# Reordering the first batch of a fused attention and gated-MLP kernel, and opening three units ahead of each block

## The chip, the cores and the metric

The kernel runs on one core of a Trainium2 chip. A core has a matrix engine (TensorE, PE in the profile, with its weight loads as PEld), a vector engine (VectorE, DVE), a scalar engine with function tables (ScalarE, ACT), a general engine (GpSimd, POOL) and a queue engine (SyncE, SP) that does nothing but issue transfers. Each works through its own instructions in order, and they wait for one another by semaphores. Sixteen DMA engines move data between the chip's memory and the on-core buffers. The metric is the device time of one execution in microseconds (us). Before the change the median of three runs is 176.78 us (176.47 to 177.16).

## The reference

Two layers, one behind the other. The first is attention over 4 batches, 8 heads, 768 positions and head width 64, in which a position sees the 128 positions up to itself and the first 4 positions of the sequence (the sinks):

```python
scores = scale * np.matmul(q, k.transpose(0, 1, 3, 2))
keep = is_sink | in_window                 # 4 sinks, window of 128
a = softmax(np.where(keep, scores, -1e9))  # over the last axis
x = np.matmul(a, v)                        # then heads side by side: (4, 768, 512)
```

The second is a gated MLP with mixing along the sequence:

```python
h = gelu_tanh(x @ w_in)                    # 512 -> 1024
u, v = h[..., :512], h[..., 512:]
v_n = (v - mean) / sqrt(var + 1e-6) * g_ln # over the 512 of v
v_s = einsum('ts,bsd->btd', w_sg, v_n) + b_sg[None, :, None]   # 768 x 768
out = x + (u * v_s) @ w_out                # 512 -> 512
```

## The kernel before

**Pairs.** The attention works on 16 pairs of heads, n = 0 to 15, four to a batch (HP = 4). For a pair, `load` (L86) brings k, q and v from memory as 32-bit floats, 384 KB each, through SP's queue; three buffers for each of the three. `cast` (L97) makes them 16-bit. `columns` (L195) turns k or q by six TensorE transposes into a PSUM bank and copies the bank out, on VectorE or ScalarE. `score(n, groups)` (L222) makes one, two or all of the pair's three groups of scores, of two key blocks each, in one of two double banks; ScalarE takes the exponential at L248. In the first four pairs, and in group 0 of pair 4, the band mask is put in beforehand: `begin_scores` (L213) fills the bank with large negative numbers by a matmul. Later pairs are masked after the exponential by `keep_band` (L250): group 0 on VectorE (L257), groups 1 and 2 on GpSimd, two selects for each group (L265, L267). `values(n, c)` (L274) multiplies one half of the pair's rows by v and divides on VectorE (L299, L300). `turn_x(n, eng)` (L304) turns the pair's result and copies it (L312 on VectorE).

**Blocks.** Behind each batch's four pairs stands a block, `hidden(b, between)` (L527). It has 14 units: six of the v half (`hidden_v`, L328), each over 128 rows, and eight of the u half (`hidden_u`, L339). A unit of the v half has four matmuls, one for each pair of the batch; `open_v` (L319) may do the first three beforehand (L325), and `hidden_v` then adds the fourth (L332), takes the gelu on ScalarE (L334) and the statistics on VectorE (L336, L337). Behind unit 7 stand `inverse_root` (L350) and the first `normalise` (L369), and one more `normalise` behind each later unit; the dictionary `between` puts other steps behind a unit of a given number. A block's later steps, `spatial` (L376: the matmuls with w_sg at L382, then L385 and L388 on VectorE) and `project` (L408), go onto the list `fillers`; `fill` takes them one by one in the pair loop of the next batch (L638 to L681), and the last batch's are taken at the end.

**Banks.** Two double banks hold scores. Four banks hold everything else (columns, values, x, hidden units, spatial, projections); a new tile gets the bank of an earlier one, and waits until that has been read.

**First batch.** Its steps are written out by hand in L554 to L634, and each engine works in that order. POOL issues the weights' loads, which turn 32-bit floats into 16-bit ones on the way: the v half of w_in (L585), the u half (L592), the two halves of w_sg (L600), and w_out (L632). So a weight is asked for when POOL has done the casts written ahead of it. SP's queue passes three gates: `hold_loads(i, behind)` (L82) issues a tiny copy that reads `behind`, so that SP waits there until `behind` has landed. The first gate stands behind w_in's v half and ahead of pair 4's k and q and of b_sg; the second behind w_in's u half and ahead of pair 4's v; the third behind w_sg's first half and ahead of pairs 5 and 6. w_sg is turned by `turn_weights` (L178): three of six columns of blocks at the end of the first block, three in the loop's first round.

Of the kernel before, what the change touches and what calls it, by code (L numbers as in the profile page):

```python
# [8 lines left out]
F32 = mybir.dt.float32  # L9
BF16 = mybir.dt.bfloat16  # L10
# [8 lines left out]
def kernel(  # L19
# [57 lines left out]

    raw = {}

    gates = consts.tile([1, 4, 16], BF16, name="gates")  # L80

    def hold_loads(i, behind):  # L82

# [13 lines left out]
    def cast(n, which, eng):  # L97
        src = raw.pop((n, which))
        if which == "v":
            eng.tensor_copy(v_bufs[n % NV][:, :, :, 0:64], src)  # L100
            return
        dst = work.tile([128, NT, 128], BF16, name=which + "_bf")
        eng.tensor_copy(dst.rearrange("p t (h d) -> p h t d", h=2), src)  # L103
        flat[n, which] = dst
# [65 lines left out]
    def turn_g():  # L170
        ps = bank([128, 512], F32, "gps")
        nc.tensor.matmul(ps[:, 0:KU], g_rows, iden4, start=True, stop=True)
        V.tensor_copy(g_sb, ps[:, 0:KU])
# [15 lines left out]
    def bank(shape, dtype, name):  # L189
        return ps_m.tile(shape, dtype, name=name, tag="m")  # L190
# [4 lines left out]
    def columns(n, which, eng):  # L195
        src = flat.pop((n, which))
        ps = bank([128, NT, 128], BF16, which + "ps")
        for t in range(NT):
            nc.tensor.transpose(ps[:, t, :], src[:, t, :], iden)  # L199
        dst = work.tile([128, S], BF16, name=which + "T")  # L200
        o, i = dst.rearrange("c (p t) -> c p t", t=NT), ps.rearrange("c t p -> c p t")
        if eng is A:
            A.copy(o, i)  # L203
        else:
            eng.tensor_copy(o, i)  # L205
        (kTs if which == "k" else qTs)[n] = dst
# [15 lines left out]
    def score(n, *groups):  # L222
        kT, qT = kTs[n], qTs[n]
        if 0 in groups:
            exps[n] = work.tile([128, HT, 1024], BF16, name="ex", bufs=3)
        for g in groups:
            if (n, g) not in scores:
                begin_scores(n, g)
            sc = scores.pop((n, g))
            w, dark = 0, darkened(n, g)  # L230
            for j in (2 * g, 2 * g + 1):
                n_q = min(256, S - 128 * j)
                for l in range(2):
                    rows = slice(64 * l, 64 * l + 64)
                    nc.tensor.matmul(sc[:, 512 * l + w:512 * l + w + n_q],  # L235
                                     kT[rows, 128 * j:128 * (j + 1)],
                                     qT[rows, 128 * j:128 * j + n_q], start=not dark,
                                     stop=not dark or j % 2 == 1)
                w += n_q
            if g == HT - 1:  # L240
                for a in range(4):
                    for l in range(2):
                        rows = slice(64 * l, 64 * l + 64)
                        nc.tensor.matmul(
                            sc[32 * a:32 * (a + 1), 512 * l + w:512 * (l + 1)], kT[rows, 0:32],
                            qT[rows, 128 * (a + 2):128 * (a + 3)], start=True, stop=True,
                            tile_position=(64 * l, 32 * a))
            A.activation(out=exps[n][:, g, :], in_=sc, func=AF.Exp, scale=scale)  # L248
# [67 lines left out]

    hvs = {}

    def open_v(b, j):  # L319
        if j == 0:  # L320
            v_alls[b] = work.tile([128, NT, DF], F32, name="v_all", tag="v_all", bufs=1)
            mvs[b] = small.tile([128, NT, 2], F32, name="mv", bufs=2)
        hvs[b, j] = bank([128, 512], F32, "hv")
        for c in range(KD - 1):
            nc.tensor.matmul(hvs[b, j], xT[b][:, c, 128 * j:128 * (j + 1)],  # L325
                             w_in_sb[:, c, DF:], start=(c == 0), stop=False)

# [240 lines left out]
    load(3, "v")  # L568


    score(0, 0, 1)
    columns(1, "k", V)
    columns(1, "q", V)
# [2 lines left out]
    cast(2, "q", G)  # L576
    score(0, 2)
    score(1, 0, 1)
    turn_g()
    columns(2, "k", A)  # L580
    columns(2, "q", V)
    cast(3, "k", G)
# [1 line left out]
    score(1, 2)  # L584
    load_w_in(slice(DF, d_ff))  # L585
    cast(1, "v", G)
    values(0, 0)
    values(0, 1)
    score(2, 0, 1)
    columns(3, "k", A)  # L590
    cast(2, "v", G)
    load_w_in(slice(0, DF))  # L592
    turn_x(0, V)
    columns(3, "q", V)
    score(2, 2)
    values(1, 0)
    values(1, 1)
    score(3, 0, 1)
    cast(3, "v", G)
    load_w_sg()  # L600
    values(2, 0)
    turn_x(1, V)
    values(2, 1)
    score(3, 2)

    hold_loads(0, w_in_sb[0:1, 0, DF:DF + 16])
    load(HP, "k")
    load(HP, "q")
    nc.sync.dma_start(out=b_bc, in_=moe_b_sg.partition_broadcast(128))
    hold_loads(1, w_in_sb[0:1, 0, 0:16])  # L610
    load(HP, "v")
    hold_loads(2, wsg_sb[0][0:1, 0, 0:16])
    for n in (HP + 1, HP + 2):
        for which in "kqv":
            load(n, which)
    cast(HP, "k", G)
    cast(HP, "q", G)
    values(HP - 1, 0)
    turn_x(HP - 2, V)
    values(HP - 1, 1)  # L620
    open_v(0, 0)
    turn_x(HP - 1, V)
    open_v(0, 1)
    cast(HP, "v", G)
    for which in "kqv":
        load(HP + 3, which)
# [11 lines left out]
    for n in range(HP, NP):  # L638
        todo = valued < n - 1
        block = n % HP == 0 and n > HP  # L640
        if HP + 3 < n + 3 < NP:
            for which in "kqv":
                load(n + 3, which)
        if n not in exps:
            score(n, 0, 1)
        if n == HP:
            for si in range(3, NT):
                turn_weights(si, V)
        keep_band(n, 0, V)
        keep_band(n, 1, G)  # L650
        if todo:
            values(n - 1, 0)
        fill(1 if todo else 2)
        if n + 1 < NP and not block:
            columns(n + 1, "k", A)
        score(n, 2)
        keep_band(n, 2, G)
        if todo:
            values(n - 1, 1)
        if QUOTA[n] > 2 and todo:  # L660
            fill()
        if n + 1 < NP and not block:
            columns(n + 1, "q", A if todo else V)
        if n + 2 < NP:
            for which in "kqv":
                cast(n + 2, which, G)
        if block:
            open_v(n // HP - 1, 0)
        if QUOTA[n] > 1:
            fill()  # L670
        if todo:
            turn_x(n - 1, V)
        if block:
            open_v(n // HP - 1, 1)
        valued = n - 1
        if block:
            hidden(n // HP - 1, {1: [lambda: values(n, 0)], 3: [lambda: values(n, 1)],
                                 5: [lambda: columns(n + 1, "k", A)], 6: [lambda: turn_x(n, V)],
                                 8: [lambda: columns(n + 1, "q", A)],
                                 LAST: [lambda: score(n + 1, 0, 1), lambda: fill(2)]})  # L680
            valued = n  # L681
    fill()
# [1 line left out]
    values(NP - 1, 1)  # L684
    fill(len(fillers) - 3)
    open_v(B - 1, 0)
    turn_x(NP - 1, V)
    open_v(B - 1, 1)
    seen = {}
    hidden(B - 1, {2: [lambda: seen.update(c=count_good())],  # L690
                   LAST: [lambda: fill(3)]})
# [42 lines left out]
```

## Time and profile before

| | us |
|---|---|
| runs, median of 3 | 176.78 |
| the profiled execution | 177.16 |
| its span | 175.3 |
| PE busy | 160.0 |
| DVE busy | 134.3 |
| ACT busy | 113.5 |
| POOL busy | 73.7 |

The span runs from the program's first instruction to its last; the execution's own time is 1.86 us longer. A row of the timeline has a start, a length, the engine, the line, the operation, the tile written and the tiles read, how many instructions it joins (x6), and in brackets how long the engine had been idle before it and who ended that. A row of the chain of waits has a start, a length and what the chain went through: an engine's instruction, a transfer (DMA), or a queue (SPq). Matmuls are pipelined, so the length of a row of matmuls has a tail beyond the moment at which the next can begin. In this execution the granted TensorE clock was 0.997 of full speed.

### The profile page before, as it was taken

The page shows a single profiled execution, that of the slowest core. Times are in us where ns is not written, and L with a number is a line of the kernel's source. Part 1 is how long each engine was busy: PE and PEld are TensorE (multiplying, and loading weights), DVE is VectorE, ACT ScalarE, POOL GpSimd, SP SyncE. Part 2 cuts the span into 40 slices and gives each one's busy share as a digit, 9 for nine tenths or more (in the row PEclk, how much of TensorE's full clock was granted, in tenths as well). Part 3 has the DMA queues.
Part 4 walks back from the last instruction along what each step waited for, and adds up shares of the span by engine and source line. Part 5 has one row for each costly group of instructions (what it writes and reads, how often), then busy time and mean ns, then how long its engine had stood idle before and what let it go on. Part 6 is the DMA issues. An engine that isn't in the chain of part 4 may idle for free.

```text
span 175.3 us, 4180 instructions
## 1 busy us (share of the span) xinstructions
PE 160.0 (91%) x1620; PEld 96.3 (55%) x1638; DVE 134.3 (77%) x322; ACT 113.5 (65%) x153; POOL 73.7 (42%) x110
## 2 busy tenths in 40 slices
PE   3989989879999999999999999999999999999960
PEld 3535654347666665565567655564676645555530
DVE  6655646997889998699689993997989979868620
ACT  2187774768986698768886875779787437621130
POOL 6344840125799989600269987000494300000000
PEclk9999999999999999999999999999999999999998
DMA  4999999998999989900099949100300130040352
GB/s 146 291 316 232 187 175 184 305 288 227 299 215 291 251 248 331 251 1 4 14 326 299 286 130 337 54 0 4 120 4 0 39 144 2 0 180 2 120 183 77
DMA packets 40355, 28.75 MB, mean 164 GB/s; under 512 B 26484, under 2 KB 37240, under 8 KB 40328
## 3 DMA queue, kind: packets, MB, share of 16 engines
q1 hardware_dynamic: 36992, 25.11, 50.7%
q0 software_dynamic: 2912, 2.77, 10.1%
q10 hardware_dynamic: 424, 0.53, 0.9%
q8 instruction: 15, 0.25, 0.6%
q14 instruction: 12, 0.10, 0.2%
HBM read 24.81 MB, written 6.29 MB: 177 GB/s over the span
## 4 chain that ended last, share of the span: by engine, by line
PE 59%; DVE 17%; DMA 13%; ACT 3%; issue 3%; POOL 1%; SPq 1%; POOLq 0%; DVEq 0%; ACTq 0%
PE vs L382 13%; PE hu L344 10%; PE o_ps L413 9%; DMA q_sb<-in_q_dram 9%; PE sc L235 5%; DMA w_in_sb<-in_moe_w_in_dram 4%; PE av L291 4%; PE hv L325 4%; DVE gv L385 3%; DVE qT L205 3%; DVE x L300 2%; DVE gT L388 2%; PE qps L199 2%; PE kps L199 2%; PE hv L332 2%
## 5 line engine op out<-in xcount | busy, mean ns | idle before, releaser
L248 ACT ACTIVATE ex<-sc 128x1024 bf16<-128x1024 f32 x48 | 47.5, 1024 | 11.7 <-PE sc L235 7.5
L382 PE MATMUL vs<-wsgT,vn 128*128 128x384 bf16 x192 | 35.3, 326 | 0.1
L265 POOL TENSOR_SCALAR_AFFINE_SELECT ex<-ex 128x512 bf16<-128x512 bf16 x24 | 16.0, 666 | 37.4 <-ACT ex L248 30.6
L382 PEld LDWEIGHTS <-vn 128*128 128x128 bf16 x192 | 17.9, 97 | 10.6 <-issue 0.3
L413 PE MATMUL o_ps<-w_out_sb,gT 128*128 128x512 bf16 x83 | 23.1, 379 | 0.5
L344 PE MATMUL hu<-xT,w_in_sb 128*128 128x384 bf16 x128 | 22.4, 326 | 0.0
L334 ACT ACTIVATE v_all<-hv 128x512 f32<-128x512 f32 x24 | 13.8, 596 | 13.0 <-PE hv L332 12.2
L385 DVE SCALAR_TENSOR_TENSOR gv<-vs,g_sb,b_bc 128x384 bf16<-128x384 f32 x32 | 19.6, 612 | 3.4 <-PE vs L382 3.1
L336 DVE BATCH_NORM_STATS2 st<-v_all 128x6 f32<-128x512 f32 x24 | 16.1, 671 | 5.0 <-ACT v_all L334 5.0
L103 POOL CAST k_bf<-k_sb 128x768 bf16<-128x768 f32 x15 | 12.7, 845 | 16.9 <-PE hu L344 10.4
L325 PE MATMUL hv<-w_in_sb,xT 128*128 128x512 bf16 x68 | 19.2, 379 | 0.5 <-DVE xT L312 0.3
L300 DVE TENSOR_TENSOR x<-av,rcps 128x384 bf16<-128x384 f32 x32 | 17.8, 557 | 1.1
L347 ACT ACTIVATE uT<-hu 128x384 bf16<-128x384 f32 x32 | 15.8, 492 | 4.2 <-PE hu L344 3.6
L388 DVE TENSOR_TENSOR gT<-gv,uT 128x384 bf16<-128x384 bf16 x32 | 16.7, 522 | 2.2 <-DVE gv L385 0.5
L422 ACT COPY o_sb<-o_ps 128x512 f32<-128x512 f32 x13 | 7.4, 593 | 14.8 <-PE o_ps L419 13.3
L235 PE MATMUL sc<-qT,kT 64*128 64x256 bf16 x192 | 15.7, 264 | 1.4 <-DVE qT L205 0.9
L103 POOL CAST q_bf<-q_sb 128x768 bf16<-128x768 f32 x15 | 14.3, 953 | 4.9 <-DMA q_sb<-in_q_dram 4.9
L344 PEld LDWEIGHTS <-w_in_sb 128*128 128x128 bf16 x128 | 12.2, 98 | 7.5
L203 ACT COPY kT<-kps 128x768 bf16<-128x768 bf16 x15 | 12.0, 799 | 6.4 <-PE kps L199 6.3
L291 PE MATMUL av<-v_sb,ex 128*128 128x65 bf16 x352 | 15.9, 194 | 0.0
L291 PEld LDWEIGHTS <-ex 128*128 128x128 bf16 x352 | 13.0, 98 | 4.1 <-issue 2.1
L100 POOL CAST v_sb<-v_sb 128x768 bf16<-128x768 f32 x15 | 13.3, 890 | 3.3 <-DMA v_sb<-in_v_dram 2.6
(90 smaller groups left out, 237.5 us busy)
## 6 DMA issues: line engine op xcount, KB each, us to landing
k_sb<-in_k_dram SPq DMA_DIRECT2D x16, 384.0 KB, 6.2
v_sb<-in_v_dram SPq DMA_DIRECT2D x16, 384.0 KB, 6.7
out_dram<-o_sb SPq DMA_DIRECT2D x23, 256.0 KB, 2.8
q_sb<-in_q_dram SPq DMA_DIRECT2D x15, 384.0 KB, 5.6
wsg_sb<-in_moe_w_sg_dram POOLq DMA_DIRECT2D x2, 576.0 KB, 11.3
w_in_sb<-in_moe_w_in_dram POOLq DMA_DIRECT2D x2, 512.0 KB, 7.5
w_out_sb<-in_moe_w_out_dram POOLq DMA_DIRECT2D x1, 512.0 KB, 9.3
q_sb<-in_q_dram ACTq DMA_DIRECT2D x1, 384.0 KB, 4.6
```

The lines of the kernel that those rows point to most:

```text
L103: eng.tensor_copy(dst.rearrange("p t (h d) -> p h t d", h=2), src)
L235: nc.tensor.matmul(sc[:, 512 * l + w:512 * l + w + n_q], kT[rows, 128 * j:128 * (j + 1)], qT[rows, 128 * j:128 * j + n_q], start=not dark, ...
L248: A.activation(out=exps[n][:, g, :], in_=sc, func=AF.Exp, scale=scale)
L291: nc.tensor.matmul(av[:, m, l, :], probs(j, l, half), v_sb[:, l, j, :], start=first, stop=False)
L300: V.tensor_mul(x_sb[b][:, hp, HT * c:HT * (c + 1), :].rearrange("p i (l d) -> p i l d", l=2), av[:, :, :, 0:64], rcp.to_broadcast([128, HT ...
L325: nc.tensor.matmul(hvs[b, j], xT[b][:, c, 128 * j:128 * (j + 1)], w_in_sb[:, c, DF:], start=(c == 0), stop=False)
L336: V.bn_stats(out=st, in_=v_alls[b][:, j, :])
L344: nc.tensor.matmul(h_ps[:, 0:NH], w_in_sb[:, c, 128 * f:128 * (f + 1)], xT[b][:, c, NH * n:NH * (n + 1)], start=(c == 0), stop=(c == KD - 1))
L382: nc.tensor.matmul(vs[:, 0:NH], vns[b][:, si, 128 * f:128 * (f + 1)], wsgT[:, si, cols], start=(si == 0), stop=(si == NT - 1))
L385: V.scalar_tensor_tensor(out=gv, in0=vs[:, 0:NH], scalar=g_sb[:, f:f + 1], in1=b_bc[:, cols], op0=ALU.mult, op1=ALU.add)
L388: V.tensor_mul(gTs[b][:, f, cols], gv, uTs[b][:, f, cols])
L413: nc.tensor.matmul(o_ps, gTs[b][:, c, rows], w_out_sb[:, c, :], start=(c == 0), stop=(c == KU - 1 and not by_act))
```

## The change

The order of the steps in the first batch is changed, and with it which transfers are asked for when:

- `score(2, 0)`, and the k columns of pair 3, stand ahead of `values(0, ...)`; `score(2, 1)` and `score(2, 2)` ahead of `values(1, ...)`, as does the first part of pair 3's scores; `turn_x(0)` stands behind the q columns of pair 3.
- `turn_x(1)` and `turn_x(2)` copy on ScalarE instead of VectorE; `turn_g` stands later.
- the load of w_in's u half stands behind the cast of pair 3's v, directly ahead of w_sg's.
- SP has two gates instead of three. The first reads pair 3's v as it was loaded, and pair 4's k, q and v and b_sg stand behind it; the second reads w_sg's first half, and pairs 5 and 6 stand behind it.
- three units of the first block are opened instead of two: the matmuls of pairs 0 and 1 for all three, then `turn_x(3)`, then those of pair 2.

In the later blocks two units are opened ahead of `turn_x` and a third behind it (before: one ahead, one behind), the filler at that place stands ahead of them, `columns(n + 1, "q")` stands behind unit 7 (before: 8), and `turn_x(n)` behind unit 9 (before: 6). The last batch's block is opened in the same way.

```diff
-    gates = consts.tile([1, 4, 16], BF16, name="gates")
+    gates = consts.tile([1, 4, 8], F32, name="gates")
...
-    def open_v(b, j):
-        if j == 0:
+    def open_v(b, j, cs=range(KD - 1)):
+        if j == 0 and 0 in cs:
...
-        hvs[b, j] = bank([128, 512], F32, "hv")
-        for c in range(KD - 1):
+        if (b, j) not in hvs:
+            hvs[b, j] = bank([128, 512], F32, "hv")
+        for c in cs:
...
+    landed = raw[3, "v"]
     score(0, 0, 1)
...
     score(1, 0, 1)
-    turn_g()
...
     load_w_in(slice(DF, d_ff))
     cast(1, "v", G)
+    score(2, 0)
+    columns(3, "k", A)
     values(0, 0)
     values(0, 1)
-    score(2, 0, 1)
-    columns(3, "k", A)
+    score(2, 1)
+    score(2, 2)
+    columns(3, "q", V)
     cast(2, "v", G)
-    load_w_in(slice(0, DF))
     turn_x(0, V)
-    columns(3, "q", V)
-    score(2, 2)
+    score(3, 0, 1)
     values(1, 0)
     values(1, 1)
-    score(3, 0, 1)
+    score(3, 2)
     cast(3, "v", G)
+    load_w_in(slice(0, DF))
     load_w_sg()
+    turn_x(1, A)
     values(2, 0)
-    turn_x(1, V)
     values(2, 1)
-    score(3, 2)
-
-    hold_loads(0, w_in_sb[0:1, 0, DF:DF + 16])
+    turn_g()
+
+    hold_loads(0, landed[0:1, 0, 0, 0:8])
     load(HP, "k")
     load(HP, "q")
+    load(HP, "v")
     nc.sync.dma_start(out=b_bc, in_=moe_b_sg.partition_broadcast(128))
-    hold_loads(1, w_in_sb[0:1, 0, 0:16])
-    load(HP, "v")
-    hold_loads(2, wsg_sb[0][0:1, 0, 0:16])
+    hold_loads(1, wsg_sb[0][0:1, 0, 0:16].bitcast(F32))
...
     values(HP - 1, 0)
-    turn_x(HP - 2, V)
     values(HP - 1, 1)
-    open_v(0, 0)
+    turn_x(HP - 2, A)
+    for j in range(3):
+        open_v(0, j, (0, 1))
     turn_x(HP - 1, V)
-    open_v(0, 1)
+    for j in range(3):
+        open_v(0, j, (2,))
...
+        if QUOTA[n] > 1:
+            fill()
         if block:
             open_v(n // HP - 1, 0)
-        if QUOTA[n] > 1:
-            fill()
+            open_v(n // HP - 1, 1)
         if todo:
             turn_x(n - 1, V)
         if block:
-            open_v(n // HP - 1, 1)
+            open_v(n // HP - 1, 2)
...
-                                 5: [lambda: columns(n + 1, "k", A)], 6: [lambda: turn_x(n, V)],
-                                 8: [lambda: columns(n + 1, "q", A)],
+                                 5: [lambda: columns(n + 1, "k", A)],
+                                 7: [lambda: columns(n + 1, "q", A)], 9: [lambda: turn_x(n, V)],
...
     open_v(B - 1, 0)
+    open_v(B - 1, 1)
     turn_x(NP - 1, V)
-    open_v(B - 1, 1)
+    open_v(B - 1, 2)
```

## The prediction

> **What bounds the kernel now.** I read the page first: its busy shares, then its DMA slices.
>
> ```profile
> span 175.3 us, 4180 instructions
> PE 160.0 (91%) x1620; PEld 96.3 (55%) x1638; DVE 134.3 (77%) x322; ACT 113.5 (65%) x153; POOL 73.7 (42%) x110
> ...
> DMA  4999999998999989900099949100300130040352
> ```
>
> TensorE is the bound, 15.3 us short of the whole span. The DMA engines are full in every slice (of 4.4 us) from the second to the ninth, that is from 4.4 to 39 us, and again later; their first gap is where the first batch ends. So I read the chain of waits in order of time for the first 45 us:
>
> ```profile
> 17.84 7.86 DMA w_in_sb<-in_moe_w_in_dram
> ...
> 25.72 0.59 SPq L84
> ...
> 27.03 9.81 DMA q_sb<-in_q_dram
> ...
> 36.99 0.84 POOL q_bf L103
> ```
>
> The chain runs through the v half of w_in (landed at 17.84 + 7.86 = 25.70), the gate behind it (L84), pair 4's q (landed at 36.84) and its cast. The timeline shows what TensorE and ScalarE wait for there; brackets hold the idle time before an instruction and who ended it:
>
> ```profile
> 17.19 1.94 ACT L248 ACTIVATE ex<-sc 128x1024 bf16<-128x1024 f32 x2 [1.00 <-PE sc L235]
> ...
> 21.77 1.94 ACT L248 ACTIVATE ex<-sc 128x1024 bf16<-128x1024 f32 x2 [0.78 <-PE sc L235]
> ...
> 24.73 1.02 ACT L248 ACTIVATE ex<-sc 128x1024 bf16<-128x1024 f32 x1 [1.02 <-PE sc L244]
> ...
> 25.80 0.24 PE L297 MATMUL av<-vsink,ex 128*128 128x65 bf16 x2 [0.74 <-ACT ex L248]
> ...
> 29.50 1.68 ACT L334 ACTIVATE v_all<-hv 128x512 f32<-128x512 f32 x3 [2.45 <-PE hv L332]
> ...
> 32.97 1.46 PE L344 MATMUL hu<-xT,w_in_sb 128*128 128x384 bf16 x8
> ...
> 35.39 0.51 PE L199 MATMUL kps<-iden,k_bf 128*128 128x128 bf16 x6 [0.96 <-POOL k_bf L103]
> ...
> 37.87 0.51 PE L199 MATMUL qps<-iden,q_bf 128*128 128x128 bf16 x6 [0.67 <-POOL q_bf L103]
> ...
> 40.82 1.17 PE L181 MATMUL wps<-iden,wsg_sb 128*128 128x128 bf16 x18
> ```
>
> After 46 us TensorE has few waits left. GpSimd's timeline shows why a gain before 45 us need not survive:
>
> ```profile
> 21.08 0.74 POOL L162 DMA_DIRECT2D w_in_sb<-in_moe_w_in_dram  x1
> ...
> 21.82 0.83 POOL L100 CAST v_sb<-v_sb 128x768 bf16<-128x768 f32 x1
> ...
> 39.56 0.85 POOL L100 CAST v_sb<-v_sb 128x768 bf16<-128x768 f32 x1 [1.75 <-DMA v_sb<-in_v_dram]
> ...
> 44.77 0.83 POOL L100 CAST v_sb<-v_sb 128x768 bf16<-128x768 f32 x1 [0.67 <-PE vs L382]
> ...
> 45.55 0.77 POOL L176 DMA_DIRECT2D w_out_sb<-in_moe_w_out_dram  x1
> ...
> 46.93 0.63 POOL L265 TENSOR_SCALAR_AFFINE_SELECT ex<-ex 128x512 bf16<-128x512 bf16 x1 [0.62 <-ACT ex L248]
> ...
> 48.54 0.64 POOL L265 TENSOR_SCALAR_AFFINE_SELECT ex<-ex 128x512 bf16<-128x512 bf16 x1 [0.28 <-PE vs L382]
> ...
> 49.51 0.94 POOL L103 CAST k_bf<-k_sb 128x768 bf16<-128x768 f32 x1
> ...
> 50.59 0.50 PE L199 MATMUL kps<-iden,k_bf 128*128 128x128 bf16 x6
> ```
>
> Pair 5's v cast at 44.77 waited for its load (the engine named had long been done). Behind it stand the issue of w_out, pair 4's band selects and pair 6's k cast, which ends at 49.51 + 0.94 = 50.45; TensorE turns that tile at 50.59. From the landing of v5 to there GpSimd idles only 0.62 + 0.28 = 0.90 us.
>
> **The change, part by part, first batch.** *Score groups ahead of values.* The three exponential waits are 1.00 + 0.78 + 1.02 = 2.80. Now score(2,0) runs while the exponential of (1,2) is under way, so the first goes; the next two shrink to an estimated 0.4 each, since score(3,0) still waits for the columns of pair 3's q. The last exponential ends near 23.8 in place of 25.75. TensorE's 0.74 goes. What is late next is the v half at 25.70, a little ahead of where the first open_v stood before. So TensorE opens the three units at about 25.9, and the first hu comes between 31.6 (everything on time) and 32.97 (nothing gained).
>
> *Two turn_x copies on ScalarE*: 0.8 each, by the nearest copy of a tile of that size (row below), inside its 2.45 of idle before the first gelu: nothing. *turn_g later*: two tiny matmuls and a copy, moved into the same stretch: nothing. *Gate shapes and one gate fewer*: one issue less on SP: nothing.
>
> ```profile
> L203 ACT COPY kT<-kps 128x768 bf16<-128x768 bf16 x15 | 12.0, 799 | 6.4 <-PE kps L199 6.3
> ...
> q_sb<-in_q_dram SPq DMA_DIRECT2D x15, 384.0 KB, 5.6
> ```
>
> *Loads held by v3.* v3 had landed by its cast at 21.82, so the gate is passed 25.72 - 21.82 = 3.9 us sooner, and SP issues k4, q4, v4 and b_bc then. Pair 4's casts come well ahead of 35.39 and 37.87, and TensorE's 0.96 + 0.67 = 1.63 go. From hu to wps takes 40.82 - 32.97 = 7.85 before, so 6.2 after: TensorE reaches wps between 37.8 and 39.2.
>
> *u half and w_sg later.* On POOL the u half now stands behind the cast of v3, that is at 22.6 in place of 21.08, and w_sg behind it, 0.74 later. What is late next is w_sg's second half:
>
> ```profile
> L168 POOL DMA_DIRECT2D wsg_sb<-in_moe_w_sg_dram x2: 738/752/767, 22.6 to 23.3; - x2
> ...
> DMA to landing us min/median/max: 7.6/9.4/13.3
> ```
>
> It landed at 23.3 + 13.3 = 36.6. Now k4, q4, v4 and b_bc go ahead of or beside it, in DMA engines that have no room. Bounds: 36.6 (not delayed), and 39.5, where before all of these loads had landed (the cast of v4 at 39.56). I take 38.5: most of them do go ahead. So wps moves from 40.82 to about 38.5, by 2.3, with 1.3 and 3.0 as ends.
>
> *What takes most of that back.* The same bytes precede v5 in the same full engines, so I hold v5 where it was, at 44.7. GpSimd then goes from its cast through w_out and four selects to k6 without its 0.90 of idle, and no sooner. TensorE waits for pair 4's selects in values(4,0) and for k6 at 50.59. So the gain after 51 us is at most 0.90; the least, if v5 comes 0.9 later, is nothing. I take 0.80: the sequence is the one on the trace, and its casts vary (0.83 to 0.94).
>
> One rule of the Trainium skill speaks against this part: "DMA: Bandwidth & Descriptors", section "Queues, rings and completion order", says each DMA engine takes turns between the queue rows that have work. By it, SP's k4 slows POOL's v half from the moment the gate opens; the 9.81 us of q4 beside w_sg, against the 5.6 that is the median of the q loads (row above), agrees. By the rule alone the v half would land about 1 us later, and the sum would come out the same, because GpSimd's bound above is the tighter.
>
> **The blocks.** The rows, at pairs 8, 12 and the last batch:
>
> ```profile
> 76.93 0.50 PE L308 MATMUL xps<-iden,x 128*128 128x128 bf16 x6
> ...
> 70.49 0.65 PE hv L325 x3
> ...
> 69.53 0.33 PE L308 MATMUL xps<-iden,x 128*128 128x128 bf16 x3
> ...
> 70.15 0.34 PE L308 MATMUL xps<-iden,x 128*128 128x128 bf16 x3 [0.29 <-DVE x L300]
> ...
> 71.14 0.11 PEld L332 LDWEIGHTS <-xT 128*128 128x128 bf16 x2 [0.50 <-DVE xT L312]
> ...
> 113.82 0.33 PE L308 MATMUL xps<-iden,x 128*128 128x128 bf16 x3
> ...
> 114.32 0.34 PE L308 MATMUL xps<-iden,x 128*128 128x128 bf16 x3 [0.17 <-DVE x L300]
> ...
> 141.17 0.59 PE L308 MATMUL xps<-iden,x 128*128 128x128 bf16 x6
> ...
> 78.39 0.53 DVE L312 COPY xT<-xps 128x768 bf16<-128x768 bf16 x1
> ...
> 78.90 3.41 PE L344 MATMUL hu<-xT,w_in_sb 128*128 128x384 bf16 x20
> ...
> 81.24 2.83 DVE L372 TENSOR_SCALAR vn<-v_all,mv,y 128x512 bf16<-128x512 f32 x6
> ```
>
> A unit's three opening matmuls take 0.65. Six transposes in a row take 0.50 with a tail of about 0.16, so three take 0.17. At pair 8 the second three start 0.62 after the first: 0.45 of waiting for x. A second unit opened ahead gives x 0.65 more: the 0.45 go. The wait for xT behind it stays, as one unit covers it before and after. At pair 12 the turn of x(12) waits 114.32 - 113.82 - 0.17 = 0.33; moved behind unit 9 it no longer does. In the last batch the six transposes took 0.59 against 0.50, and the xT copy queued behind an output add; I take 0.16 for both, with 0 and 0.3 as ends. Sum 0.45 + 0.33 + 0.16 = 0.94. Opening a unit ahead delays the first gelu of the block by 0.65 - 0.45 = 0.2; VectorE's normalised tiles still end (81.24 + 2.83 = 84.07) ahead of the spatial matmuls behind two projections, so nothing. The fill that moves ahead of open_v does the same work earlier: nothing. The q transposes at unit 7 instead of 8: same work, nothing.
>
> **Sum.** The profiled execution took 177.16 (span 175.3 and 1.86 around it), 0.38 over the median of 176.78. 177.16 - 0.80 - 0.94 = 175.42; against the median, 175.04.
>
> **Rivals.** *(a) GpSimd does not bind*, because v5 lands sooner or its selects do: then w_sg's landing and VectorE's wsgT copies set the shift, 1.3 to 2.3, and the time is 176.78 - 0.94 - 1.8, about 174.0. For it: SP passes its last gate with less in its queue. Against: the DMA share shows no free engine before 40 us.
>
> *(b) The first batch gives nothing*: v5 lands 0.9 or more later, since k5's gate now waits behind w_sg's first half, which itself stands later. Time 176.78 - 0.94 = 175.8. For it: w_sg asked 0.74 later. Against: v4 and b_bc keep SP's queue filled meanwhile.
>
> *(c) Slower: the bank of the late turn.* turn_x behind unit 9 puts its copy on VectorE behind the inverse root and three normalisations. Without the copy ahead, normalising starts at 81.24 - 0.53 = 80.7; three take 1.42, the copy 0.53: the PSUM bank is free at 82.7. The last hu unit starts at 78.90 + 4 x 0.65 = 81.5, less 0.45. If it is given that bank, one of four, TensorE waits 1.6 in each of two blocks: 175.04 + 3.2 = 178.2. It decides when this unit, not one after it, gets the bank. Against: the other three banks come back as soon as a gelu has read them, and a bank that is free sooner may be taken first.
>
> *(d) w_sg's second half lands after 42.5*, with everything SP asked ahead of it: the first batch then loses 1.7 and more, 177.5.
>
> **How the numbers follow.** Forecast 0.52; (a) 0.13; (b) 0.18; (c) 0.10; (d) 0.07: GpSimd's idle is on the trace, while (a), (c) and (d) each need an order of transfers or banks that no row shows. A change of 0.5%, 0.9 us, is about what this measurement can tell: faster is below 175.9, slower above 177.66. The forecast's own range is 174.4 to 175.8. The forecast, but for 0.02 at its edge, and (a) are faster; (b) lies at the bound, and 0.06 of it is faster, 0.12 same; (c) is slower; (d) is split. That makes faster 0.69, same 0.18, slower 0.13. The range runs from 173.8, just below (a), to 177.0, between (b) and (d); it leaves out (c), most of (d) and a little of (a), 0.19 in all.
>
> **What would show it.** Right: no wait above 0.3 at the exponentials of pair 2, k4 and q4 transposes without wait, wps starting near 38.5 and behind a wsg landing, a wait of TensorE for GpSimd between 46 and 51 us, the k6 transposes near 49.8, and no wait for x at pairs 8 and 12. Wrong: wps later than 40 us, v5's cast away from 44.8, or a hu unit that waits for VectorE's xT copy near 81 or 118 us.

## The result, and the profile after

The changed kernel takes 174.83 us (median of 6 runs), the kernel before 176.84 on the same chip: a ratio of 0.9881, with a 95% interval from 0.9856 to 0.9905. By this ratio it is faster by 2.1 us. The ratio, like those below, leaves out executions that took well over the kernel's shortest (here one of the six, 179.34 at a granted clock of 0.979, where the others had 0.991 to 0.998), so the two medians lie a little less apart, 2.0. The profiled execution took 174.74. The head of its page:

```profile
span 173.0 us, 4178 instructions
PE 160.5 (93%) x1621; PEld 96.9 (56%) x1638; DVE 132.6 (77%) x320; ACT 114.1 (66%) x155; POOL 74.5 (43%) x110
```

TensorE's busy time is nearly the same (160.0 before) and the span is 2.3 shorter. The timeline of ScalarE and TensorE in the first batch, after the change (start, length, engine, line, what, and in brackets the idle time before it and who ended it; `...` marks rows left out; lines from L325 on are one higher here than before):

```profile
18.16 1.94 ACT L248 ACTIVATE ex<-sc 128x1024 bf16<-128x1024 f32 x2 [0.31 <-PE sc L235]
20.98 1.94 ACT L248 ACTIVATE ex<-sc 128x1024 bf16<-128x1024 f32 x2 [0.88 <-PE sc L235]
23.61 1.02 ACT L248 ACTIVATE ex<-sc 128x1024 bf16<-128x1024 f32 x1 [0.69 <-PE sc L244]
...
29.69 1.57 ACT L335 ACTIVATE v_all<-hv 128x512 f32<-128x512 f32 x3 [0.76 <-PE hv L333]
...
26.63 1.64 PE L326 MATMUL hv<-w_in_sb,xT 128*128 128x512 bf16 x5
...
32.51 1.46 PE L345 MATMUL hu<-xT,w_in_sb 128*128 128x384 bf16 x8
33.81 0.50 PE L199 MATMUL kps<-iden,k_bf 128*128 128x128 bf16 x6
...
35.44 0.50 PE L199 MATMUL qps<-iden,q_bf 128*128 128x128 bf16 x6
...
38.38 1.17 PE L181 MATMUL wps<-iden,wsg_sb 128*128 128x128 bf16 x18
...
43.49 2.22 PE L383 MATMUL vs<-wsgT,vn 128*128 128x384 bf16 x9 [1.37 <-DVE wsgT L186]
...
50.11 0.50 PE L199 MATMUL kps<-iden,k_bf 128*128 128x128 bf16 x6
```

Pair 4's k and q are turned without a wait, and TensorE is at wps 2.44 ahead of before (38.38 against 40.82). Then it waits 1.37 for VectorE's copies of w_sg, and at pair 6's k transposes only 0.48 is left (50.11 against 50.59). This wait stands where before had none. What VectorE and GpSimd do there, after the change:

```profile
37.66 3.93 DVE L373 TENSOR_SCALAR vn<-v_all,mv,y 128x512 bf16<-128x512 f32 x6
...
41.82 0.82 DVE L146 COPY mask<-mask 128x512 bf16<-128x512 bf16 x1
...
42.95 1.41 DVE L186 COPY wsgT<-wps 128x768 bf16<-128x768 bf16 x3
...
40.48 0.83 POOL L103 CAST k_bf<-k_sb 128x768 bf16<-128x768 f32 x1 [1.13 <-DMA k_sb<-in_k_dram]
41.67 0.83 POOL L103 CAST q_bf<-q_sb 128x768 bf16<-128x768 f32 x1 [0.36 <-PE wps L181]
43.31 0.83 POOL L100 CAST v_sb<-v_sb 128x768 bf16<-128x768 f32 x1 [0.81 <-DMA v_sb<-in_v_dram]
...
47.93 0.64 POOL L265 TENSOR_SCALAR_AFFINE_SELECT ex<-ex 128x512 bf16<-128x512 bf16 x1 [1.84 <-PE vs L383]
```

And before, with TensorE's first opened unit:

```profile
26.75 0.38 PE L325 MATMUL hv<-w_in_sb,xT 128*128 128x512 bf16 x1
...
38.26 3.33 DVE L372 TENSOR_SCALAR vn<-v_all,mv,y 128x512 bf16<-128x512 f32 x6
...
41.83 0.29 DVE L146 COPY mask<-mask 128x512 bf16<-128x512 bf16 x1
...
43.44 1.49 DVE L186 COPY wsgT<-wps 128x768 bf16<-128x768 bf16 x3 [0.94 <-PE wps L181]
```

Before, VectorE waited 0.94 for TensorE's wps; now it comes to w_sg's copies straight from its own masks, 0.49 ahead of before. GpSimd casts pair 5's v at 43.31 in place of 44.77, and idles 1.84 ahead of its second pair of selects: no wait for what it hands over holds the first batch.

The blocks after the change, on the timeline of TensorE and VectorE:

```profile
69.42 0.50 PE L308 MATMUL xps<-iden,x 128*128 128x128 bf16 x6
...
78.38 2.76 PE L345 MATMUL hu<-xT,w_in_sb 128*128 128x384 bf16 x16
81.08 0.61 PE L235 MATMUL sc<-qT,kT 64*128 64x256 bf16 x8
...
140.35 0.50 PE L308 MATMUL xps<-iden,x 128*128 128x128 bf16 x6
...
81.74 0.55 DVE L312 COPY xT<-xps 128x768 bf16<-128x768 bf16 x1
```

At pair 8 the six transposes come in one piece where before they came three and three; in the last batch they take 0.50 in place of 0.59. The copy of the late turn is at 81.74, behind three normalised tiles; by then the units of hu have run through without a gap.

To see where time goes, I compare the starts of the same ScalarE instructions in two traces: the first exponential of a pair, and the last copy of an output. The table says how many us each kernel is ahead of the kernel before at these places (+: behind). The labels are those of the experiments; "after" is the changed kernel as it was first measured (the expectations call this the first look), and e13 is the same kernel again.

| start in the kernel before | 44.9 (pair 4) | 49.2 (pair 5) | 55.2 (pair 6) | 66.3 (pair 8) | 84.2 (pair 9) | 121.4 (pair 13) | 168.4 (last copy) |
|---|---|---|---|---|---|---|---|
| after | 2.44 | 0.48 | 0.48 | 0.76 | 1.17 | 1.46 | 1.75 |
| e13, the same kernel again | 2.55 | 1.18 | 1.18 | 1.46 | 1.87 | 2.17 | 2.46 |
| e1, first batch alone | 2.62 | 0.87 | 0.77 | 1.01 | 1.23 | 1.22 | 1.35 |
| e2, blocks alone | 0.80 | 0.09 | 0.09 | 0.09 | 0.50 | 0.80 | 0.96 |
| e4, two units opened | 2.51 | 1.76 | +0.52 | +0.24 | 0.17 | 0.47 | 0.76 |
| e10, and product from PSUM | 2.44 | 2.36 | 1.96 | 2.18 | 2.59 | 2.50 | 2.32 |
| e11, GpSimd waits | 2.13 | 1.54 | 1.43 | 1.67 | 2.08 | 2.38 | 2.66 |
| e12, PSUM but in the last batch | 2.13 | 2.05 | 0.33 | 0.28 | 0.69 | 0.60 | 0.68 |
| e5, old gates | 0.73 | 0.73 | 0.73 | 1.01 | 1.42 | 1.72 | 2.01 |
| e9, old order of scores | 2.54 | 1.12 | 1.12 | 1.12 | 1.53 | 1.83 | 1.99 |
| e15, old gates, PSUM | 0.13 | 0.15 | 0.15 | 0.34 | 0.75 | 0.66 | 0.74 |

Two traces of one kernel differ by 0.7 between pairs 4 and 5 and then keep that difference to the end. From pair 13 to the last copy "after" gains 0.29: 0.16 is there at the first output behind the last block (at 152.85 before, 151.23 after), and 0.13 comes behind that, in e1 too, whose last block is as before. One trace shows where time goes; what a part is worth is read from the times.

### The profile page after: what moved, and what is told of

It is laid out like the page before. It is cut to its first block, busy times and chain, and to the rows that moved or that the text cites. A ratio compares the mean times of both kernels' runs of the same rounds, so it can differ in the third digit from the quotient of the medians.

```text
span 173.0 us, 4178 instructions
## 1 busy us (share of the span) xinstructions
PE 160.5 (93%) x1621; PEld 96.9 (56%) x1638; DVE 132.6 (77%) x320; ACT 114.1 (66%) x155; POOL 74.5 (43%) x110
## 4 chain that ended last, share of the span: by engine, by line
PE 78%; DVE 14%; issue 2%; POOL 1%; ACT 1%; POOLq 0%; DVEq 0%; ACTq 0%
PE vs L383 15%; PE o_ps L414 11%; PE hu L345 9%; PE hv L326 8%; PE av L291 7%; PE sc L235 7%; PE xps L308 3%; PE hv L333 3%; DVE qT L205 3%; PE kps L199 3%; PE qps L199 2%; PE sc L218 2%; DVE vn L373 2%; PE av L297 2%; DVE st L337 2%
## 5 line engine op out<-in xcount | busy, mean ns | idle before, releaser
L335 ACT ACTIVATE v_all<-hv 128x512 f32<-128x512 f32 x24 | 13.3, 599 | 11.3 <-PE hv L333 10.0
L326 PE MATMUL hv<-w_in_sb,xT 128*128 128x512 bf16 x68 | 18.7, 379 | 0.3
L300 DVE TENSOR_TENSOR x<-av,rcps 128x384 bf16<-128x384 f32 x32 | 17.8, 557 | 1.1
L100 POOL CAST v_sb<-v_sb 128x768 bf16<-128x768 f32 x15 | 14.0, 934 | 9.2 <-DVE vn L373 6.8
```

The lines of the kernel that those rows point to most:

```text
L300: V.tensor_mul(x_sb[b][:, hp, HT * c:HT * (c + 1), :].rearrange("p i (l d) -> p i l d", l=2), av[:, :, :, 0:64], rcp.to_broadcast([128, HT ...
```

## Experiments

The expectations speak of theories V, G, P and R. V: VectorE's chain, from the first gelu over statistics, inverse root, normalised tiles and masks to w_sg's copies, sets the first batch's end. G: GpSimd's casts and selects do, as in the prediction. P: VectorE's instructions with both inputs in on-core buffers wait out GpSimd's. R: such a long instruction waits for something else.

**The two halves of the change.** e1 is the changed kernel with the later blocks as before; e2 is the kernel before with the blocks changed.

```diff
 e1
-            open_v(n // HP - 1, 0)
-            open_v(n // HP - 1, 1)
+        if block: open_v(n // HP - 1, 0)     # fill() and turn_x(n - 1, V) behind it, then open_v(.., 1)
-        7: columns(n + 1, "q"), 9: turn_x(n, V)
+        6: turn_x(n, V), 8: columns(n + 1, "q")
```

> The first batch as changed, the later blocks as before. Theory V (VectorE's chain from the first gelu over statistics, inverse root, normalising and masks to its wsgT copies sets the first batch's end): pair 6's k transposes at 50.1 us as in the changed kernel, TensorE waiting about 1.4 us for VectorE's wsgT copies, the time 0.5 to 0.8 under before. Theory G (the prediction's: GpSimd's casts and selects set it): the same place, reached by a wait for GpSimd, 0.8 under before. If the parts do not add, the time is at that of before or at that of the changed kernel.

> The first batch as before, the blocks of pairs 8, 12 and of the last batch as changed. The prediction's sum for these is 0.94 us (0.45 at pair 8, 0.33 at pair 12, 0.16 at the end): 175.9 where before has 176.8, a ratio of 0.9947. The rival that the late turn's bank holds up the last hu unit would give 1.6 us of waiting in each of two blocks, a time above before.

Measured: e1 0.988 (0.9847 to 0.9913), e2 0.9937 (0.9914 to 0.996). The blocks alone give 1.1 us by the times, and in the table the gains at pair 8's block, pair 12's and the last are 0.41, 0.30 and 0.15. The first batch alone gives 2.1, more than its expectation (0.5 to 0.8) and as much as the whole change; in its trace pair 6's k transposes come at 49.72, behind a wait of 0.86 for w_sg's copies, so theory V named the wait, but not its size. So the two don't add up in the times: what the blocks give on top of the first batch lies within the intervals, and isn't settled by them. In e1's trace part of it is there already. Its TensorE timeline at pair 8:

```profile
68.52 0.74 PE L308 MATMUL xps<-iden,x 128*128 128x128 bf16 x6
```

That is 0.24 longer than six transposes without a wait (0.50); before, the wait was 0.45. With the first batch changed it is smaller.

**What holds VectorE: masks, and the third unit.** e3 makes the band masks (L144 to L147) ahead of the block and not between the normalised tiles and w_sg's copies; e4 opens two units in the first block.

```diff
 e3
-    band_masks()                    # behind load_w_out()
+    band_masks()                    # behind turn_x(HP - 2, A)
 e4
-    for j in range(3):              # open_v(0, j, ...), both times
+    for j in range(2):
```

> The changed kernel with the building of the band masks (three VectorE instructions, 1.4 us at 41.5 us) moved to VectorE's idle time ahead of the turn of pair 3. Theory V: the wsgT copies start about 1.3 us sooner, pair 6's k transposes come near 48.8 us, the time is 1.3 us under the changed kernel's (about 173.5 where that has 174.8). Theory G: GpSimd does not move, the transposes stay at 50.1 us and the time at 174.8.

> The changed kernel with two units of the first block opened instead of three. Theory V: the first gelu starts at about 29.1 us instead of 29.7, VectorE's whole chain with it, and the time falls by about 0.6 us, although TensorE has one opened unit less under its wait for the last turn. If opening the third unit pays in TensorE's time, as the change has it, the time rises by 0.2 to 0.6 us instead.

Measured: e3 0.985 (0.9822 to 0.9878, on four of its twelve runs), e4 0.9864 (0.9827 to 0.9902). The times settle neither: for e3 theory V asked for about 0.981 and G for 0.988, and both lie just outside the interval; e4 lies below the changed kernel, but within the intervals. e3 is judged by its times alone. The trace of e4 shows VectorE's chain moved as theory V says, and then something new. Its timeline, by engine:

```profile
28.97 1.68 ACT L335 ACTIVATE v_all<-hv 128x512 f32<-128x512 f32 x3 [0.32 <-PE hv L333]
...
41.12 1.40 DVE L186 COPY wsgT<-wps 128x768 bf16<-128x768 bf16 x3
...
47.51 3.67 DVE L389 TENSOR_TENSOR gT<-gv,uT 128x384 bf16<-128x384 bf16 x1
...
47.43 0.81 POOL L103 CAST k_bf<-k_sb 128x768 bf16<-128x768 f32 x1
48.19 0.82 POOL L103 CAST q_bf<-q_sb 128x768 bf16<-128x768 f32 x1
48.96 0.82 POOL L100 CAST v_sb<-v_sb 128x768 bf16<-128x768 f32 x1
49.74 0.63 POOL L265 TENSOR_SCALAR_AFFINE_SELECT ex<-ex 128x512 bf16<-128x512 bf16 x1
50.33 0.63 POOL L267 TENSOR_SCALAR_AFFINE_SELECT ex<-ex 128x512 bf16<-128x512 bf16 x1
51.21 1.06 POOL L265 TENSOR_SCALAR_AFFINE_SELECT ex<-ex 128x512 bf16<-128x512 bf16 x1 [0.26 <-ACT ex L248]
...
52.53 1.15 PE L383 MATMUL vs<-wsgT,vn 128*128 128x384 bf16 x6 [2.11 <-DVE x L300]
```

Without the third unit the first gelu is 0.72 sooner (28.97 against 29.69), and w_sg's copies begin 1.83 sooner (41.12 against 42.95). Only a part of this is the unit's. From the start of the first opened unit to the first gelu e4 takes 2.62 (from 26.35), and e10, e11, e12 and e15, also with two units, take 2.62 or 2.63; the changed kernel takes 3.06 (from 26.63), and so does e13. So the third unit costs VectorE's chain 0.44, and it saves TensorE a wait of 0.22 for the copy of x, which e4 has at 28.55. The other 0.28 of the 0.72 e4 has gained before any unit is opened, with the same order of steps. The rest of the 1.83 is VectorE's own: six normalised tiles in 3.33 in place of 3.93, the mask copy in 0.29 in place of 0.82.

At pair 5 e4 is 1.28 further ahead than the first trace of the changed kernel. Then one product gT, which takes 0.36 at its shortest, takes 3.67. Under it GpSimd runs five instructions without a break, and the product ends (51.18) when GpSimd has its first idle time (50.96 to 51.21). TensorE waits 2.11 for VectorE's division (L300), which stands behind the product, and all of the lead is gone. This execution took 175.66; five of e4's runs took 174.14 to 174.71, so such a product need not be in most of them.

**Is it GpSimd?** In e10 gv is written over vs in PSUM, so that the product has one input from a buffer and one from PSUM. In e11 GpSimd reads the product before it begins pair 6's casts, so that it can't run beside it. Both open two units.

```diff
 e10
-        gv = small.tile([128, NH], BF16, name="gv")
+        gv = vs[:, 0:NH]
 e11 (loop, n == 4)
+            fill()                                          # moved from behind the casts
+            G.tensor_copy(seen_gT, gTs[0][0:1, 2, 0:8])
             for which in "kqv": cast(n + 2, which, G)
```

> The changed kernel with two units opened in the first block, as in the run with two opens, and gv (L386) written over vs in its PSUM bank instead of into a buffer on the core, so that the product gT (L389) has one input from a buffer and one from PSUM. In the run with two opens one product took 3.67 us from 47.51, while GpSimd ran selects and casts with no idle time from 43.60 to 50.96, and TensorE then waited 2.11 us. Theory P (a VectorE instruction with both inputs in buffers waits out GpSimd's instructions, several in a row): no product over 1.0 us any more; TensorE's 2.11 go; pair 6's q transposes come at about 51.5 in place of 53.52; against that stands a product from PSUM of 0.5 to 0.65 in place of 0.36 to 0.8. Ratio 0.980 (0.975 to 0.985). Theory R (the product waits for something else, such as uT or its semaphore): a product of more than 2 us stays near 47.5, and the ratio stays 0.986 or goes up.

> The changed kernel with two units opened in the first block, and in the loop's first round a GpSimd copy of 8 numbers that reads the third gT, ahead of GpSimd's casts of pair 6: GpSimd waits until VectorE has made that product, and does its casts after it. Theory P: the product of 3.67 us takes 0.36 to 0.8; the k cast of pair 6 begins at about 47.9 in place of 47.43 and TensorE turns that tile at about 49.0 in place of 48.83; the next VectorE instruction with both inputs in buffers is the mask product of pair 5 (L257), and it may be held in its turn, by at most the casts and selects behind it, 2.4 us. Ratio 0.980 if it isn't held, 0.988 if it is. Theory R: the product stays above 2 us, the casts come behind it, at 51.2, and the ratio is 0.998 or more.

The product gT in the view by tile (shortest, median, longest, in ns), first e4, then e10:

```profile
L389 DVE TENSOR_TENSOR gT<-gv,uT x32: 357/424/3667, 43.7 to 165.3; 128x384 bf16<-128x384 bf16 x32
```

```profile
L389 DVE TENSOR_TENSOR gT<-vs,uT x32: 556/557/558, 43.7 to 163.6; 128x384 bf16<-128x384 f32 x32
```

With one input in PSUM, all 32 products take the same to 2 ns, whatever GpSimd does: it works without a break in e10 too, from 45.02 past 52. In e11's timeline:

```profile
47.73 0.36 DVE L389 TENSOR_TENSOR gT<-gv,uT 128x384 bf16<-128x384 bf16 x1
...
48.15 0.18 POOL L672 COPY seen_gT<-gT 1x8 bf16<-1x8 bf16 x1 [0.46 <-DVE gT L389]
```

The product that took 3.67 takes 0.36 when GpSimd stands still, and e11 is 1.43 ahead at pair 6 where e4 was 0.52 behind. Theory R falls by e10's trace: beside a GpSimd without a break no product is long, and none even varies, where the changed kernel's take 0.36 to 0.82. P agrees with all of this. e11's product agrees too, but alone it could be chance, since the two traces of the changed kernel have none above 0.82 either. By the times the gain that P promised (0.980) did not come: e11 has 0.9864 (0.9821 to 0.9907), as e4 has, and two runs of e10, 174.47 and 175.03 (before: 177.02), are too few for an interval and would give 0.986 and 0.989.

**The same in the rest.** e12 is e10 with the last batch's product from a buffer again; e13 is the changed kernel once more, measured beside e12; e14 is the kernel before with e12's edit.

```diff
 e12, e14
-        gv = small.tile([128, NH], BF16, name="gv")
+        gv = vs[:, 0:NH] if b < B - 1 else small.tile([128, NH], BF16, name="gv")
```

> As the run with two opens and the product from PSUM, but the last batch keeps its product from a buffer (0.36 there, where GpSimd does nothing, against 0.56 from PSUM). That run's profile was 2.59 us ahead of before at 152 us and lost 0.26 of it behind. Theory P: nothing is lost there, span 172.2 to 172.5, ratio 0.981 (0.976 to 0.986), below the changed kernel of the same call by about 0.006. Theory R (GpSimd's instructions have no part in it): ratio as the changed kernel's, 0.988.

> The changed kernel once more, beside the version with two opens and the product from PSUM. Both theories: ratio 0.988 (0.985 to 0.991). Theory P: its products between 43 and 56 us differ in length from the first look's (0.81, 0.36, 0.36), since it is chance in which order they meet GpSimd's instructions; each costs 0.36 or up to 1 us, and one of more than 3 us may appear. Theory V: VectorE's mask copies and wsgT copies end near 44.3 and TensorE waits for them for about 1.4 us, as in the first look.

> The kernel before, with gv written over vs in PSUM in all batches but the last. Theory P: every product of the first three batches takes about 0.56; in the kernel before those between 46 and 56 us took 0.36 to 0.72, mean 0.52, so there is next to nothing to gain: ratio 0.997 to 1.001. What holds VectorE up ahead of them (six normalised tiles, masks, wsgT) is as it was, and pair 6's k transposes come at 50.3 to 50.6. Theory R: the same ratio. A ratio below 0.994 would say that the kernel before lost time to GpSimd as well, which its trace doesn't show.

Measured: e12 0.9898 (0.9867 to 0.9928), e13 0.9896 (0.9854 to 0.9938), e14 1.0017 (0.9989 to 1.0044). e14 came out as expected, within its interval: the kernel before lost nothing measurable to the product. The 0.981 for e12 was a miss, and its trace, of one of its longer executions (175.98), shows one way in which time was lost:

```profile
48.19 2.73 DVE L257 TENSOR_TENSOR ex<-ex,mask 128x1024 bf16<-128x1024 bf16 x1 [0.48 <-ACT ex L248]
...
50.32 1.10 POOL L265 TENSOR_SCALAR_AFFINE_SELECT ex<-ex 128x512 bf16<-128x512 bf16 x1
...
51.68 1.15 PE L383 MATMUL vs<-wsgT,vn 128*128 128x384 bf16 x6 [1.21 <-DVE x L300]
```

The next VectorE instruction with two inputs in buffers, the mask product of pair 5, took the product's place: 2.73, where its shortest in this trace is 0.68, beneath three casts of GpSimd; then a select of GpSimd was held in its turn (1.10, where others take 0.63). Here the wait was not removed, it moved one instruction on. e13's trace has the chain of "after" with smaller stalls: its six normalised tiles took 3.34 in place of 3.93, w_sg's copies begin at 42.23, and TensorE waits 0.76 for them, not the 1.4 expected.

**Gates and scores.** e5 has SP's three gates and the u half's place as before, e9 the order of scores and values as before, with `turn_x`'s copies on VectorE and the early `turn_g` (the rest as changed), e15 is e12 with e5's edit.

```diff
 e5, e15
+    load_w_in(slice(0, DF))                     # ahead of cast(3, "v", G), not behind it
+    hold_loads(0, w_in_sb[0:1, 0, DF:DF + 16])  # then k, q of pair 4 and b_sg
+    hold_loads(1, w_in_sb[0:1, 0, 0:16])        # then v of pair 4
+    hold_loads(2, wsg_sb[0][0:1, 0, 0:16])      # then pairs 5 and 6
 e9
+    values(0, 0); values(0, 1); score(2, 0, 1); columns(3, "k", A); ...   # lines of before
```

> The changed kernel with SP's three gates, and w_in's u half asked for ahead of the cast of pair 3's v, as before; scores, opened units and blocks as changed. Pair 4's k and q then land as before, and TensorE waits for their casts: first wps at about 40 in place of 38.4. Theory V (VectorE's chain from the first gelu to the wsgT copies sets the first batch's end): that chain is as in the changed kernel, wsgT is copied at about 43, pair 6's k transposes come at 50.1 to 50.3; ratio 0.988. Theory G (GpSimd, from the landing of pair 5's v): v5 is cast at 44.7 as before, k transposes at 50.5; ratio 0.990 to 0.991. Theory P: either, with up to 2 us more or less by where VectorE's products fall among GpSimd's instructions between 46 and 52 us.

> The changed kernel with the order of scores, columns, values and turn_x of before in the first batch (copies on VectorE, turn_g early), and the loads' order, gates, opened units and blocks as changed. The three waits for exponentials of 0.8 to 1.0 come back and the last exponential ends at about 25.7. Theory V: the v half of w_in lands at 25.4 in both, so the first gelu stays near 29.6 to 30 and the first batch ends 0 to 0.3 later than in the changed kernel; ratio 0.988 to 0.990. If the order of the scores made the gain, pair 6's k transposes fall back to 50.6 and the ratio is 0.992 or more. Theory P: as V, with up to 2 us by where VectorE's products fall.

> As the version with two opens and the product from PSUM in all batches but the last, with SP's three gates and the place of w_in's u half as before. The run with the old gates (2.0 us ahead of before in its profile, but 0.9 us ahead by its times) left open what the gates are worth. Without products held up by GpSimd: pair 4's k and q cast later, first wps at about 40.1 in place of 38.4, VectorE's wsgT copies at 42.5 as in the version with the new gates, so TensorE comes to pair 6's k transposes 1.0 to 1.7 later, at 49.2 to 49.9. Ratio 0.988 (0.984 to 0.992), 0.006 to 0.007 above the version with the new gates. If VectorE's chain alone set the end, the two would be within 0.002.

Measured: e5 0.9948 (0.9927 to 0.997), e9 0.9931 (0.9905 to 0.9958), e15 0.9979 (0.9959 to 0.9999). Against the changed kernel's 0.988 to 0.990 e5 is 0.5 to 0.7% slower, and e15 is 0.8% slower than e12, measured beside it, with intervals apart: the gates, with the place of the u half, are worth about 1 us. Theories V and G both gave them less, and e15's own figure (0.988) was a miss, though its distance to e12 was not. The order of the scores would be worth 0.4 to 0.5% by e9, but e9's interval meets that of "after" and overlaps e13's, so this is not settled. e5's TensorE and VectorE timelines show the mechanism of the gates:

```profile
35.16 0.51 PE L199 MATMUL kps<-iden,k_bf 128*128 128x128 bf16 x6 [1.22 <-POOL k_bf L103]
...
40.09 1.17 PE L181 MATMUL wps<-iden,wsg_sb 128*128 128x128 bf16 x18
...
36.41 0.69 DVE L365 TENSOR_TENSOR s<-y 128x6 f32<-128x6 f32 x1
```

The waits for pair 4's k come back and wps is 1.71 later. Pair 4's late q cast (POOL, 36.26) also falls on VectorE's inverse root and stretches one of its small instructions from 0.17 to 0.69. e15's trace, of a typical execution (176.43, median 176.54), has the same: waits of 0.61 and 1.01 for pair 4's k and q, and wps at 40.69 where e12 has 38.69; at pair 4 it is 0.13 ahead where e12 is 2.13. For e9 I have no such line. TensorE's wait of 0.74 for an exponential is back (at 25.73), but its first gelu is at 29.59, no later than in the changed kernel, pair 6's k transposes come at 49.47 and not at the 50.6 of the alternative, and its trace is 1.99 ahead at the end. The executions profiled of e5 and e9 were the shortest of their runs, 175.03 and 175.18 where the medians are 176.08 and 175.94; so neither trace shows what the longer runs lost. Where that goes is open.

No version is shown to beat the changed kernel: e3, e4 and e11 lie 0.002 to 0.005 below it, within the intervals.

## Why the prediction was right, and where it was not

**Right by the total, in part by luck.** 175.0 was forecast and 174.83 measured. The blocks' half of the sum had its mechanism right; the first batch's half had not, and its size came near that of a different mechanism.

**Exponentials and scores.** The wait at score(2,0) went, but 0.31 stands at (2,1); the next, 0.78, grew to 0.88, and 1.02 became 0.69. So 2.80 became 1.88 and not 0.8, and the last exponential ends at 24.63 in place of 23.8 forecast. The first hu came at 32.51, between the ends given, but not in the way given: the forecast had TensorE wait for w_in's v half and open the units at 25.9. It opened the first at 26.63 (before: 26.75), after matmuls without a wait since 20.49.

**The v half and the rule of the Trainium skill.** The tile view of the changed kernel has the two loads of w_in:

```profile
L162 POOL DMA_DIRECT2D w_in_sb<-in_moe_w_in_dram x2: 740/757/774, 17.5 to 22.3; - x2
...
DMA to landing us min/median/max: 8.0/8.2/8.4
```

The v half landed between 25.5 and 25.9 (25.70 before). The prediction drew about 1 us of delay, without a working, from the Trainium skill, "DMA: Bandwidth & Descriptors", section "Queues, rings and completion order". This trace shows no such delay: from its issue the v half took 8.0 or 8.4 where before it took 7.86. In other traces with the same gate it took 7.5 or 7.8 (e13) and 6.4 or 7.2 (e4). TensorE did not wait for it: in e4 it had landed by 24.7, and the first unit opened at 26.35.

**wps** was forecast at 38.5 and came at 38.38, with k4 and q4 without a wait: the gate was passed at 21.48, 4.24 sooner than before (3.9 forecast), and this part of the mechanism is as given. The reason given for its place was wrong: w_sg's second half landed at 37.6 (issued at 23.7, 13.9 to landing), and TensorE came straight from the hu units.

**"What takes most of that back" is the step that failed.** It held pair 5's v at 44.7, made GpSimd the bound, and from this took 0.80, with 0.90 as the most possible. Pair 5's v was cast 1.46 sooner (43.31, a sign of being wrong that the prediction itself had named), GpSimd had idle time to spare, and e10, with all of its GpSimd work, was 1.96 ahead at pair 6. What takes the gain back in the traces is VectorE, which had 0.94 of idle time ahead of w_sg's copies before, and then no more. First, its chain does not start sooner: the first gelu is at 29.69 (29.50 before), since TensorE comes to the first unit only 0.12 sooner and the third unit costs 0.44. The prediction counted opened units as a cost in later blocks only, and there at nothing. Second, GpSimd stands in VectorE's way, but not through what it hands over: while it works, some of VectorE's instructions wait. In "after" the six normalised tiles and the mask copy took 0.60 and 0.53 longer than before; before, the inverse root had lost 0.65 in the same way (an instruction of 0.82 in place of 0.17, at 37.01). That price was nowhere in the sum. So w_sg's copies came 0.49 sooner, and 0.48 was left at pair 6. That VectorE's 0.94 lies so near the 0.90 of GpSimd, from which the 0.80 came, is luck. In e13 1.18 was left, and in both traces 0.28 more came between pairs 7 and 8. By the times of e1 the first batch gave about 2.1, not 0.80; as its share and that of the blocks do not add, I don't divide the total further.

**The blocks.** Forecast 0.45, 0.33 and 0.16; "after" has 0.41, 0.29 and 0.16, and e2, which has no other edit, 0.41, 0.30 and 0.15. The mechanism (a second unit covers x, a later turn meets a finished x) is as given.

**Rivals.** (a) named the right engine at the right instruction, w_sg's copies on VectorE, but its shift of 1.3 to 2.3 was too large for the traces of the changed kernel (0.48 and 1.18), while the 2.1 of e1's times lies within it. (b) is refuted by e1. (c) is refuted by the trace: the copy came at 81.74, no hu unit waited. (d) is refuted as well: w_sg's second half landed at 37.6.

**Not explained.** Why the first batch is worth 2.1 by e1's times and 0.5 to 1.2 in the traces of the changed kernel at pair 6 is open. The span shrank by 2.3 and the last copy moved by 1.75; the rest lies in the last store and behind, where both kernels do the same.

## What to carry to other kernels

When a wait is taken off the bounding engine, follow each of the other engines through the same stretch from its own first input: the gain here stopped at VectorE, whose chain began no sooner. An operation moved ahead to cover one wait delays what stood behind it; in the first block the third opened unit saved TensorE 0.22 and cost VectorE's chain 0.44. A difference between two traces is not yet the edit's: of the 0.72 between e4 and the changed kernel 0.28 stood ahead of the place where they differ. And two engines that exchange no data may still stop each other: look for an instruction whose longest row is several times its shortest, and lay the other engine's rows under it.

## What was not expected of the hardware

A VectorE instruction with both inputs in on-core buffers waited behind GpSimd's casts and selects, and not behind one only: 3.67 us in place of 0.36 beneath five of them without a break, 2.73 in place of 0.68 beneath three. With one input in PSUM the product took 0.556 to 0.558 in 32 of 32 cases. The Trainium skill, "SBUF — State Buffer", section "Who interferes with whom", says that such an instruction contends with a GpSimd instruction that reads buffers; section "SBUF: two separate sides" says that whichever starts first keeps the shared ports for its whole instruction. The products from PSUM agree. If a wait were over with the instruction under way, the product would have taken at most about 1.2 (an estimate: 0.36 and a cast of 0.82); here several instructions followed one another while VectorE waited. In other places it was served between two of them; what decides that, no run here shows. Small instructions pay the same price: 0.69 in place of 0.17 in the inverse root. Two inputs are not the only condition, either: the mask copy, with one input, took 0.82 in place of 0.29 beside a cast, and in the same trace one of the 24 normalised tiles 1.13 where the shortest took 0.53. No run here separates what these need.
